# Attention, top-2 experts and a gated feed-forward on one core: sums of gathered outputs on POOL, one token tile's gathers behind the branch, a transpose a step later, and some norm products on ACT

## The chip, the cores and the metric

One core of a Trainium2 chip runs the whole program. Its engines run beside each other, each through its own list of instructions in order: PE (TensorE, matmuls), DVE (VectorE), ACT (ScalarE), POOL (GpSimd) and SP (SyncE, which mostly issues DMAs). They wait for one another by semaphores. The metric is the device time of one execution in microseconds (us), the median of the runs.

## The reference, cut to what matters

```python
# 1. linear attention: 4 batches, 8 heads, 576 positions, 64 per head
kv  = einsum('bhsd,bhse->bhde', k, v)
out = einsum('bhsd,bhde->bhse', q, kv)
x   = out / sqrt(mean(out*out, -1) + 1e-6) * g_norm      # per head
x   = x as 2304 tokens of 512
# 2. eight experts, two for each token
noisy = x @ w_gate + log1p(exp(x @ w_noise)) * noise
top2, w = the two largest of noisy, softmax over the two
y = sum over the two of  w * (relu(x @ w1[e]) @ w2[e])   # 512 -> 1024 -> 512
# 3. a gated feed-forward, 512 -> 1536 -> 512
g = y @ w_gate2
return (g * sigmoid(g) * (y @ w_val)) @ w_out
```

## The kernel before, in words

**Numbers.** Each float32 operand of a large product is split in a high and a low half (names with hi_/lo_, xh/xl, mh/ml, hh/hl, gh/gl), and three matmuls (hi·hi, hi·lo, lo·hi; `three_terms`) take the place of one. ACT makes the high halves, DVE the low ones (lo = value - hi).

**Stages.** The attention (`front`, per batch) leaves unnormalised outputs xo in tiles of 128 tokens, 18 in all. `route_norm` computes the norms ny per token and head on DVE, and POOL multiplies xo by them into xs (L387, two instructions for a row of 128 tokens) and, for the last nine tiles (g = 2), issues the stores of xs to xd in DRAM (L393). Then routing chooses two experts for each token and gives each of its rows a slot (slot_tok).

The experts run in 14 blocks of 256 or 384 rows, eight steps each; a step is one `expert_up` (u), one `expert_act` (hh, hl) and the `expert_down` (y) of the step before. In the first 16 steps the routing of the last nine tiles (`chain`) is woven between the tasks of the steps by `weave`, piece by piece, and PE, ACT, DVE and SP keep the order in which the program is written (PINNED); from step 16 on a scheduler of the compiler orders them. So a different number of instructions in `chain`, or another task in a step, moves where `weave` cuts. A dictionary of tasks says what else is done in a step: `at(step, fn)`. Rows of a block are gathered from xd by POOL's indirect DMAs (`x_gather`, L703); blocks 0 to 3 are transposed by PE (tr, in `x_halves`), later ones by DVE (`turn`, behind a store and a load that reorder quarters: `to_quarters`, L720 and L721).

The feed-forward runs in six groups m of three token tiles, twelve units each: `ffn_up` (ug, uv; sg, a, gh, gl) and `ffn_down` (y('m', m)). For each token tile t, `y_mix` gathers the two expert rows ya and yb from yd (POOL), `y_sum` weights and adds them, and puts the sum out in quarters (yq); `y_get` reads it back; `y_halves` transposes it (`turn` on DVE) and makes mh on ACT and ml on DVE. The gathers of t < 3 read only the rows of the first blocks of each expert.

**The branch.** After unit 1 of the feed-forward, `spill` loads the number of rows that found no slot (toti, L878) into a register on each engine, and each engine branches by it (L879) past a body that handles such rows. With these inputs it is passed. Each engine passes it when it comes to it in its own list.

**Lines.** L387/L393 norm products and stores; L703 gathers; L622 raw weights from DRAM; L630 hi_, L984 lo_ of weights; L669 POOL's adds in the conversion of feed-forward weights (36 in the expert steps); L806 ACT's ya times weight; L807 DVE's yb times weight plus ya; L834 ug and uv; L776 y; L766/L767 hh/hl; L44 is the line of everything recorded in the pinned stretch.

Of the kernel before, what the change touches and what calls it, by code (L numbers as in the profile page):

```python
# [15 lines left out]
AF = mybir.ActivationFunctionType  # L16
OP = mybir.AluOpType
# [32 lines left out]
def attn_moe_ffn(ctx: ExitStack, tc: tile.TileContext, q, k, v, g_norm, w_gate, w_noise, noise, w1, w2,  # L50
                 u_gate, u_val, u_out, out):
    nc = tc.nc
    PE, ACT, V, POOL, SP = (InOrder(tc, e) for e in (nc.tensor, nc.scalar, nc.vector, nc.gpsimd, nc.sync))
    B, H, S, D = q.shape
    NTOK, DM = out.shape
# [3 lines left out]
    P = 128  # L59
# [16 lines left out]
    xd = dram.tile([NTOK, DM], F32, name="xd")  # L76
# [5 lines left out]
    def wtile(nm):  # L82
        return wpool.tile([P, 1024], F32, name=nm, tag="W")
# [22 lines left out]
    def const(shape, dt, nm):  # L106
        return consts.tile(shape, dt, name=nm)
# [64 lines left out]
    wts = const([P, NT, 2], F32, "wts")  # L172
# [182 lines left out]
    def small(shape, nm, dt=F32, most=5):  # L355
        full = [shape[0], most] + shape[2:]
        tag = nm.split("@")[0]
        return pool.tile(full, dt, name=nm, tag="sm_" + tag.split("_")[0], bufs=2 if tag[:2] == "ny" else 1)[:, 0:shape[1]]

    def route_norm(g):  # L360
        ts = list(range(*GRP[g]))
        G = len(ts)
        m = small([P, G, H], f"m@{g}", most=TP)
        V.tensor_scalar(m, SS[g], 1.0 / D, EPS_RMS, op0=OP.mult, op1=OP.add)
        yield
        t1 = small([P, G, H], f"nt@{g}", most=TP)
        V.tensor_scalar(t1.bitcast(I32), m.bitcast(I32), 1, None, op0=OP.logical_shift_right)
        yield
        y = small([P, G, H], f"ny@{g}", most=TP)
        V.tensor_scalar(y.bitcast(I32), t1.bitcast(I32), -1, SEED, op0=OP.mult, op1=OP.add)  # L370
        yield
        for it in range(3):
            V.tensor_mul(t1, y, y)
            yield
            V.scalar_tensor_tensor(t1, t1, -0.5, m, op0=OP.mult, op1=OP.mult)
            yield
            V.scalar_tensor_tensor(y, t1, 1.5, y, op0=OP.add, op1=OP.mult)
            yield
        for t, xo in XO.pop(g):
            n = xo.shape[1]  # L380
            xs = wtile(f"xs{t}")
            for r in range(n):
                xi = xo[:, r].rearrange("p (c s) (l i) -> p c s l i", s=2, i=32)
                xp = xs[:, r * DM:(r + 1) * DM].rearrange("p (s l c i) -> p c s l i", s=2, l=2, i=32)
                yr = y[:, t - ts[0] + r].rearrange("p (c s) -> p c s", s=2)
                for s in range(2):
                    POOL.tensor_mul(xp[:, :, s], xi[:, :, s], yr[:, :, s, None, None].to_broadcast([P, 4, 2, 32]))  # L387
            store = partial((SP if g < 2 else POOL).dma_start, xd[t * P:(t + n) * P].rearrange("(r p) d -> p r d", r=n),
                            xs[:, 0:n * DM].rearrange("p (r d) -> p r d", r=n))
            if g < 2:  # L390
                XO.setdefault(g, []).append(store)
            else:
                store()  # L393
        RT["y", g] = y

    def route_logits(g):
        t0, t1 = GRP[g]
        G = t1 - t0
        y = RT.pop(("y", g))
        lg, az = small([P, G, 16], f"lg@{g}", most=TP), small([P, G, E], f"az@{g}", most=TP)  # L400
        for b in (g,) if g < 2 else (2, 3):
            ts = slice(PART[b][0] - t0, PART[b][1] - t0)
            lz = ZO[b].rearrange("p g h n -> p (g h) n")
            V.tensor_mul(lz, lz, y[:, ts].rearrange("p g h -> p (g h)")[:, :, None].to_broadcast([P, lz.shape[1], 16]))
            yield BIG
            V.tensor_reduce(lg[:, ts], ZO[b].rearrange("p g h n -> p g n h"), op=OP.add, axis=AX.X)
            yield BIG
        zn = lg[:, :, 8:16]
        V.scalar_tensor_tensor(az, zn, -1.0, zn, op0=OP.mult, op1=OP.max)
        yield  # L410
        RT["lg", g] = lg, az
# [306 lines left out]
    def to_quarters(x, nm):  # L718
        put, get = by_quarter(nm)
        SP.dma_start(put, x.rearrange("p (g k) -> p g k", g=4))  # L720
        return lambda: SP.dma_start(x, get)  # L721
# [81 lines left out]

    def y_sum(t):
        a, b = XT.pop(("y", t))
        ACT.activation(a, a, AF.Copy, scale=wts[:, t, 0:1])  # L806
        V.scalar_tensor_tensor(b, b, wts[:, t, 1:2], a, op0=OP.mult, op1=OP.add)  # L807
        XT["y", t] = b, to_quarters(b, f"yq{t}")

    def y_get(t):  # L810
# [166 lines left out]
    def at(step, fn, *args):  # L977
        todo.setdefault(step, []).append((fn, args))
# [35 lines left out]
    for bk in range(2, NB):  # L1014
        p = starts[bk - 1]
        n = blocks[bk][2] // P
        for i in range(n):
            if bk > 2:
                at(p + 1 if bk < 4 else p - 4, x_gather, bk, i)
            if bk > 3:  # L1020
                at(p - 2 + i, x_put, bk, i)
                at(p + 1 + i, x_get, bk, i)
            at(p + (5 if bk == 2 else 4) + i, x_halves, bk, i)
    for m in range(NM):
        p = first_ffn + NU * (m - 1) if m else first_ffn - NF - 4
        for i in range(3):
            lags = [2 * i + d for d in (1, 3, 4, 7)] if m else [i + d for d in (0, 4, 6, 8)]
            for lag, fn in zip(lags, (y_mix, y_sum, y_get, y_halves)):
                at(p + lag, fn, 3 * m + i)

# [17 lines left out]
    def front(b):  # L1048
# [61 lines left out]
        if b < 2:  # L1110
            drain(route_norm(b), route_logits(b))
# [29 lines left out]
    def chain():  # L1141
        yield from route_norm(2)
        yield from route_logits(2)
        yield STOP
        yield BIG
        yield from route_top(2)
        yield from route_rank(2)
        yield from route_rows(2)
        yield from slot_hits(2)
        yield from late_sum()  # L1150
        for i in range(3):
            x_gather(2, i)

    def weave(gen, tasks, budget):

        spent = 0
        for i, task in enumerate(tasks + [lambda: None]):
            while spent < budget * (i + 1) / (len(tasks) + 1):
                spent += next(gen, STOP) or 2
            task()  # L1160

    at(PINNED, mix_weights)
    at(PINNED + 1, y_rows)
    for i in range(2):
# [77 lines left out]
```

## Time and profile before

| what | value |
|---|---|
| runs | 1019.26 us median of 3 (1015.68 to 1022.33) |
| the profiled execution | 1018.99 us, span 1017.3 us |
| mean granted clock of PE | 0.991 |
| busy share of PE, DVE, ACT, POOL | 97%, 55%, 35%, 18% |
| PE's idle time put down to other work, three longest single waits | 3.7, 3.6, 2.1 us |

The span is the time from the first to the last instruction in the trace; 1.7 us of the execution lie around it. Idle time of an engine carries the name of what ended it. A queue name with q (ACTq, PEq) is the engine's sequencer: register loads, branches, DMA issues.

### The profile page before, as it was taken

To read this page: it belongs to the slowest core of one execution; us is meant where nothing else is said; L and a number is where in the kernel's file an instruction comes from. 1 tells how busy PE (TensorE), PEld (TensorE's weight loads), DVE (VectorE), ACT (ScalarE), POOL (GpSimd) and SP (SyncE) were. 2 spreads that over 40 slices of the span, in tenths; PEclk is the share of its full clock that TensorE was granted. 3 is DMA by queue.
4 is the path that set the end of the run, shared out by engine and by line. 5 is a ranking of instruction groups with operands and counts; after the bars stand their busy time and mean duration, and the time that the engine had idled before them with its cause. 6 is when DMAs were issued, how large, how long until landed. Compare 5 with 4: busy or idle time off the path is not lost. (4 is left out here: it accounts for less than half of the span.)

```text
span 1017.3 us, 14793 instructions
## 1 busy us (share of the span) xinstructions
PE 985.5 (97%) x5719; PEld 899.1 (88%) x5720; DVE 564.0 (55%) x1080; ACT 351.6 (35%) x620; POOL 181.4 (18%) x171
## 2 busy tenths in 40 slices
PE   7997899999999999999999899999999999999998
PEld 7885788888989899898889799999999999999997
DVE  1879879877847776678466442522522522522222
ACT  4653434443426253542156321411411411411211
POOL 2416152233121313014120320200200200000000
PEclk9989999999999999999999999999999999999999
DMA  9987678688857768676472620400500500300000
GB/s 249 302 243 199 216 249 287 208 310 259 284 187 226 243 211 284 199 220 208 149 232 95 187 84 1 145 11 1 149 8 1 155 2 1 93 1 1 32 1 32
DMA packets 114508, 151.61 MB, mean 149 GB/s; under 512 B 15936, under 2 KB 75328, under 8 KB 114432
## 3 DMA queue, kind: packets, MB, share of 16 engines
q1 hardware_dynamic: 99536, 113.51, 36.6%
q0 software_dynamic: 6736, 22.29, 7.2%
q10 hardware_dynamic: 8160, 14.81, 4.0%
q8 instruction: 46, 0.75, 0.3%
q14 instruction: 30, 0.25, 0.1%
HBM read 108.64 MB, written 41.94 MB: 148 GB/s over the span
## 5 line engine op out<-in xcount | busy, mean ns | idle before, releaser
L840 DVE TENSOR_TENSOR sg<-ug,sg 128x384 f32<-128x384 f32 x72 | 40.0, 555 | 181.5 <-ACT sg L839 181.4
L757 PE MATMUL u<-xl,hi_w 128*128 128x384 f32 (+1 forms) x448 | 140.4, 313 | 0.0
L757 PE MATMUL u<-xh,lo_w 128*128 128x384 f32 (+1 forms) x448 | 140.3, 313 | 0.0
L757 PE MATMUL u<-xh,hi_w 128*128 128x384 f32 (+1 forms) x448 | 140.2, 313 | 0.0
L776 PE MATMUL y<-hi_w,hh 128*128 128x512 f32 x290 | 115.3, 398 | 2.0 <-ACT hh L766 1.8
L776 PE MATMUL y<-lo_w,hh 128*128 128x512 f32 x290 | 115.0, 396 | 0.0
L834 PE MATMUL ug<-mh,hi_ug 128*128 128x384 f32 x288 | 97.4, 338 | 3.7 <-ACTq L879 3.7
L766 ACT ACTIVATE hh<-u 128x384 fp32r<-128x384 f32 (+1 forms) x113 | 49.4, 438 | 147.6 <-PE u L757 145.3
L834 PE MATMUL ug<-mh,lo_ug 128*128 128x384 f32 x288 | 97.6, 339 | 0.0
L834 PE MATMUL ug<-ml,hi_ug 128*128 128x384 f32 x288 | 97.2, 338 | 0.0
L839 ACT ACTIVATE sg<-ug 128x384 f32<-128x384 f32 x72 | 35.4, 491 | 177.4 <-PE ug L834 175.8
L834 PE MATMUL uv<-mh,lo_uv 128*128 128x384 f32 x288 | 96.6, 335 | 0.0
L776 PE MATMUL y<-hi_w,hl 128*128 128x512 f32 x290 | 95.5, 399 | 1.2 <-DVE hl L767 1.0
L834 PE MATMUL uv<-mh,hi_uv 128*128 128x384 f32 x288 | 96.5, 335 | 0.0
L834 PE MATMUL uv<-ml,hi_uv 128*128 128x384 f32 x288 | 96.4, 335 | 0.0
L757 PEld LDWEIGHTS u<-xl,hi_w 128*128 128x128 f32 x448 | 84.7, 189 | 5.7
L757 PEld LDWEIGHTS u<-xh,lo_w 128*128 128x128 f32 x448 | 84.6, 189 | 5.0
L757 PEld LDWEIGHTS u<-xh,hi_w 128*128 128x128 f32 x448 | 84.6, 189 | 4.6
L843 ACT ACTIVATE gh<-a 128x384 fp32r<-128x384 f32 x72 | 37.8, 525 | 145.5 <-DVE a L841 145.5
L767 DVE SCALAR_TENSOR_TENSOR hl<-u,hh 128x384 fp32r<-128x384 f32 (+1 forms) x113 | 56.0, 496 | 56.2 <-ACT hh L766 56.2
L841 DVE TENSOR_TENSOR a<-uv,sg 128x384 f32<-128x384 f32 x72 | 40.1, 556 | 59.6 <-PE uv L834 59.6
L984 DVE TENSOR_TENSOR lo_w<-raw_w,hi_w 128x1024 fp32r<-128x1024 f32 x48 | 59.8, 1246 | 22.2 <-ACT hi_w L630 20.9
(421 smaller groups left out, 2010.3 us busy)
## 6 DMA issues: line engine op xcount, KB each, us to landing
raw_w<-in_moe_w_dram SPq DMA_DIRECT2D x56, 512.0 KB
yd<-ys ACTq DMA_DIRECT2D x40, 256.0 KB
xq<-xg SPq DMA_DIRECT2D x30, 256.0 KB
xg<-xq SPq DMA_DIRECT2D x30, 256.0 KB
d_ug<-in_moe_w_gate_dram SPq DMA_DIRECT2D x12, 512.0 KB
d_uv<-in_moe_w_val_dram SPq DMA_DIRECT2D x12, 512.0 KB
d_uo<-in_moe_w_out_dram SPq DMA_DIRECT2D x12, 512.0 KB
yq<-yb SPq DMA_DIRECT2D x18, 256.0 KB
```

Source lines behind the costliest of these rows:

```text
L757: PE.matmul(pu, w[a][:, c, (f % 2) * P:(f % 2 + 1) * P], xs[b][:, c, 0:n], start=(k == 0), stop=(k == 11))
L766: ACT.activation(hi.bitcast(F32R), pu, AF.Relu)
L767: V.scalar_tensor_tensor(lo.bitcast(F32R), pu, 0.0, hi, op0=OP.max, op1=OP.subtract)
L776: PE.matmul(ACC[key][i], hs[a][:, i * P:(i + 1) * P], w[b][:, fi], start=(f == 0 and k == 0), stop=(f == nf - 1 and k == 2), skip_group_ch ...
L834: PE.matmul(pu, w[a][:, c, (f % 2) * P:(f % 2 + 1) * P], xs[b][:, c], start=(k == 0), stop=(k == 11))
L839: ACT.activation(sg, ps[0], AF.Sigmoid)
L840: V.tensor_mul(sg, ps[0], sg)
L841: V.tensor_mul(a, ps[1], sg)
L843: ACT.activation(hi.bitcast(F32R), a, AF.Copy)
L984: at(step + 1, lambda: V.tensor_sub(*late.pop()))
```

## The change

Four parts. (1) In `route_norm` for g = 2, tiles 15 (two rows of 128 tokens) and 17 (one row) are no longer multiplied by POOL. `scale_later` queues 24 ACT instructions, one for a row and head (128x64, the norm as its scale operand), and behind each tile's the store by POOL; `scale_some` issues up to five of these items in each of the steps 5 to 12 (the first come in step 6). (2) In `y_sum` ACT's and DVE's instruction give way to three of POOL: two products by the weight as a pointer scalar, and an add. (3) The lags of the feed-forward's tasks for m >= 1 go from (1, 3, 4, 7) to (2, 4, 5, 7), so that the gathers of t = 3, which read all of yd, stand behind the branch. (4) The transposes of block 2 go from steps 13, 14, 15 to steps 14, 15, 15.

```diff
+            if g == 2 and t > 13:
+                at(5 if t == 15 else 9, scale_later, t, xo, y[:, t - ts[0]:t - ts[0] + n], n)
+                continue
...
+    def scale_later(t, xo, y, n):
+        xs = wtile(f"xs{t}")
+        todo_of = []
+        for r in range(n):
...
+            for h in range(H):
+                todo_of.append(partial(ACT.activation, xp[:, h // 2, h % 2], xi[:, h // 2, h % 2], AF.Copy,
+                                       scale=y[:, r, h:h + 1]))
+        todo_of.append(partial(POOL.dma_start, xd[t * P:(t + n) * P].rearrange("(r p) d -> p r d", r=n),
+                               xs[:, 0:n * DM].rearrange("p (r d) -> p r d", r=n)))
+        SCALES.extend(todo_of)
...
+    def scale_some():
+        for fn in SCALES[:5]:
+            fn()
+        del SCALES[:5]
...
     def y_sum(t):
         a, b = XT.pop(("y", t))
-        ACT.activation(a, a, AF.Copy, scale=wts[:, t, 0:1])
-        V.scalar_tensor_tensor(b, b, wts[:, t, 1:2], a, op0=OP.mult, op1=OP.add)
+        for c, y in ((0, a), (1, b)):
+            POOL.tensor_scalar(y, y, wts[:, t, c:c + 1], None, op0=OP.mult)
+        POOL.tensor_add(b, b, a)
...
-            at(p + (5 if bk == 2 else 4) + i, x_halves, bk, i)
+            at(p + (min(6 + i, 7) if bk == 2 else 4 + i), x_halves, bk, i)
...
-            lags = [2 * i + d for d in (1, 3, 4, 7)] if m else [i + d for d in (0, 4, 6, 8)]
+            lags = [2 * i + d for d in (2, 4, 5, 7)] if m else [i + d for d in (0, 4, 6, 8)]
...
+    for step in range(5, 13):
+        at(step, scale_some)
```

**DVE in step 5** of the expert steps: the low half of a weight piece, then the routing chain's polynomial (ac) around hl_4, the low half that PE's y of that step takes. Before:

```order
L44 TENSOR_TENSOR s2@2_1352<-s@2_1350 128x72
L44 TENSOR_TENSOR lo_w_0_3_1360<-raw_w_0_3_1167,hi_w_0_3_1359 128x1024
L44 TENSOR_SCALAR ac@2_1363<-s2@2_1352 128x72
L44 SCALAR_TENSOR_TENSOR ac@2_1363<-ac@2_1363,s2@2_1352 128x72 x4
L44 SCALAR_TENSOR_TENSOR hl_4_1389<-u_4_1333,hh_4_1388 128x256
L44 SCALAR_TENSOR_TENSOR ac@2_1363<-ac@2_1363,s2@2_1352 128x72 x2
```

and with the change:

```order
L44 TENSOR_TENSOR s2@2_1342<-s@2_1340 128x72
L44 TENSOR_TENSOR lo_w_0_3_1350<-raw_w_0_3_1167,hi_w_0_3_1349 128x1024
L44 TENSOR_SCALAR ac@2_1353<-s2@2_1342 128x72
L44 SCALAR_TENSOR_TENSOR ac@2_1353<-ac@2_1353,s2@2_1342 128x72 x3
L44 SCALAR_TENSOR_TENSOR hl_4_1378<-u_4_1323,hh_4_1377 128x256
L44 SCALAR_TENSOR_TENSOR ac@2_1353<-ac@2_1353,s2@2_1342 128x72 x3
```

One of the four ac instructions ahead of hl_4 has moved behind it.

**ACT before the branch**, from the last store of the expert blocks (ys) on; sg_1 and gh_1 are the sigmoid and the high half of unit 1 of the feed-forward. Before:

```order
L789 DMA yd<-ys_1_6001 128x512
L839 ACTIVATE sg_1_6030<-ug_1_6004 128x384
L843 ACTIVATE gh_1_6035<-a_1_6031 128x384
L806 ACTIVATE ya_6040<-ya_6040,wts 128x512
L878 TENSOR_LOAD toti
L879 COMPARE_AND_BRANCH
```

and with the change:

```order
L812 DMA yd<-ys_1_6022 128x512
L863 ACTIVATE sg_1_6051<-ug_1_6025 128x384
L867 ACTIVATE gh_1_6056<-a_1_6052 128x384
L902 TENSOR_LOAD toti
L903 COMPARE_AND_BRANCH
```

The product of the gathered ya of t = 3 no longer stands ahead of ACT's branch.

**POOL around the sums of m = 0** (t = 0 to 2), up to the branch. Before:

```order
L703 DMA ya_5616<-yd,posi 128x512
L703 DMA yb_5617<-yd,posi 128x512
L703 DMA ya_5649<-yd,posi 128x512
L703 DMA yb_5650<-yd,posi 128x512
L703 DMA ya_6040<-yd,posi 128x512
L703 DMA yb_6041<-yd,posi 128x512
L878 TENSOR_LOAD toti
```

and with the change:

```order
L726 DMA ya_5667<-yd,posi 128x512
L726 DMA yb_5668<-yd,posi 128x512
L830 TENSOR_SCALAR ya_5597<-ya_5597,wts 128x512
L830 TENSOR_SCALAR yb_5598<-yb_5598,wts 128x512
L830 TENSOR_SCALAR ya_5634<-ya_5634,wts 128x512
L830 TENSOR_SCALAR yb_5635<-yb_5635,wts 128x512
L830 TENSOR_SCALAR ya_5667<-ya_5667,wts 128x512
L830 TENSOR_SCALAR yb_5668<-yb_5668,wts 128x512
L831 TENSOR_TENSOR yb_5598<-yb_5598,ya_5597 128x512
L831 TENSOR_TENSOR yb_5635<-yb_5635,ya_5634 128x512
L831 TENSOR_TENSOR yb_5668<-yb_5668,ya_5667 128x512
L902 TENSOR_LOAD toti
```

All six products stand ahead of the first add, and the two gathers of t = 3 are gone from ahead of the branch. On DVE the transposes of the three sums (turn) stand later than before: the first directly ahead of the hl_4 of the last expert block, the other two behind it, ahead of its hl_5; before, all three stood behind its hl_0.

## Rows read from the trace of the kernel before

**Rows 1.** page part 1: busy time, its share of the span, instructions

```profile
PE 985.5 (97%) x5719; PEld 899.1 (88%) x5720; DVE 564.0 (55%) x1080; ACT 351.6 (35%) x620; POOL 181.4 (18%) x171
```

**Rows 2.** waits of PE: awaited, then total us, times, longest us

```profile
PE y L44 <- DVE hl L44: 7.5, 7, 3.6
PE ug L834 <- ACTq L879: 3.7, 1, 3.7
...
PE tr L44 <- DMA xg<-xd,slot_tok: 2.1, 1, 2.1
PE y L776 <- ACT hh L766: 1.8, 1, 1.8
```

**Rows 3.** windows: each engine's busy us and count, PEclk (granted clock), DMA share, GB/s

```profile
100.70:104.20 3.50, 3.46 (x12) 3.09 (x13) 3.36 (x12) 0.00 (x0) 3.48 (x6) 0.51 0.71 267
...
150.00:500.00 350.00, 348.90 (x1867) 313.50 (x1866) 262.17 (x445) 136.64 (x202) 90.15 (x62) 1.00 0.74 238
...
525.90:531.00 5.10, 5.09 (x20) 4.34 (x21) 5.10 (x8) 3.57 (x5) 0.00 (x0) 0.67 0.63 177
...
571.40:575.40 4.00, 3.95 (x14) 3.95 (x15) 1.71 (x2) 1.06 (x2) 2.36 (x2) 0.57 0.88 255
575.40:1015.00 439.60, 437.27 (x2298) 408.60 (x2296) 154.45 (x257) 107.95 (x188) 28.89 (x27) 1.00 0.15 46
```

**Rows 4.** timeline of DVE: start, us, work [idle before, what ended it]

```profile
85.06 0.23 DVE L44 SCALAR_TENSOR_TENSOR ny@2_1197<-nt@2_1193,ny@2_1197 128x72 f32<-128x72 f32 x1
...
95.85 1.64 DVE L44 TENSOR_TENSOR lo_w<-raw_w,hi_w 128x1024 fp32r<-128x1024 f32 x1
...
98.06 2.29 DVE L44 SCALAR_TENSOR_TENSOR ac@2_1363<-ac@2_1363,s2@2_1352 128x72 f32<-128x72 f32 x4
100.27 0.41 DVE L44 SCALAR_TENSOR_TENSOR hl<-u,hh 128x256 fp32r<-128x256 f32 x1
...
544.91 0.43 DVE L767 SCALAR_TENSOR_TENSOR hl<-u,hh 128x256 fp32r<-128x256 f32 x1
```

**Rows 5.** timeline of POOL

```profile
86.32 13.94 POOL L387 TENSOR_TENSOR xs<-xo,ny@2_1197 128x256 f32<-128x256 f32 x17 [16.12 <-ACT hh L44]
...
126.82 1.03 POOL L703 DMA_INDIRECT xg<-xd,slot_tok  x1 [22.47 <-DVE slot_tok L44]
...
343.28 3.23 POOL L669 TENSOR_TENSOR f_uv<-f_uv,d_uv 128x512 f32<-128x512 f32 x1 [11.52 <-DVE d_uv L668]
...
518.98 1.05 POOL L703 DMA_INDIRECT yb<-yd,posi  x1 [0.30 <-issue]
```

**Rows 6.** timeline of ACT

```profile
105.38 1.57 ACT L44 ACTIVATE xh<-tr,ghalf 128x256 fp32r<-128x256 f32 x4 [8.24 <-PE tr L44]
...
523.93 0.72 ACT L806 ACTIVATE ya<-ya,wts 128x512 f32<-128x512 f32 x1 [3.21 <-DMA ya<-yd,posi]
...
570.38 0.72 ACT L806 ACTIVATE ya<-ya,wts 128x512 f32<-128x512 f32 x1 [5.67 <-DMA ya<-yd,posi]
572.50 1.06 ACT L630 ACTIVATE hi_ug<-raw_ug 128x1024 fp32r<-128x1024 f32 x1 [1.41 <-DMA raw_ug<-ug]
```

**Rows 7.** timeline of PE, where block 2's inputs are transposed

```profile
132.74 0.66 PE L44 MATMUL tr<-ident,xg 128*128 128x128 f32 x4 [2.09 <-DMA xg<-xd,slot_tok]
```

**Rows 8.** timeline of SP's queue, behind the branch

```profile
567.87 0.37 SPq L622 DMA_DIRECT2D raw_ug<-ug  x1
...
571.91 0.36 SPq L720 DMA_DIRECT2D yq<-yb  x1
...
574.65 0.33 SPq L721 DMA_DIRECT2D yb<-yq  x1
```

**Rows 9.** groups by form: count, busy us, mean ns, idle before and its releasers

```profile
L669 POOL TENSOR_TENSOR f_ug<-f_ug,d_ug 128x512 f32<-128x512 f32 x12 | 22.6, 1890 | 43.5 <-DVE d_ug L668 26.8 <-issue 16.6
...
L168 POOL MEMSET rb<- 128x1280 f32 x4 | 4.5, 1155 | 0.0
...
L44 ACT ACTIVATE zo<-o 128x64 f32<-128x64 f32 x12 | 4.0, 335 | 0.0
```

More of the change, by code (lines that the diff above doesn't have):

```diff
@@ L394, in route_norm @@
         RT["y", g] = y
+    def scale_later(t, xo, y, n):
+        xs = wtile(f"xs{t}")
+        todo_of = []
+        for r in range(n):
+            xi = xo[:, r].rearrange("p (c s) (l i) -> p c s l i", s=2, i=32)
+            xp = xs[:, r * DM:(r + 1) * DM].rearrange("p (s l c i) -> p c s l i", s=2, l=2, i=32)
+            for h in range(H):
[4 more added lines that the diff above has]
+        SCALES.extend(todo_of)
+    SCALES = []
+    def scale_some():
+        for fn in SCALES[:5]:
+            fn()
+        del SCALES[:5]
     def route_logits(g):
```

## The prediction

> **What bounds the kernel now.** I read the busy shares first: PE works in 97% of the span [rows 1], so the kernel ends when PE's list ends, and only PE's idle time and its clock can give anything back. The windows say where there is nothing to find: in 150 to 500 us PE is busy in 348.90 of 350 us, and in 575.4 to 1015 us in 437.27 of 439.6, both at a granted clock of 1.00 [rows 3]. What ACT and DVE lose to POOL's sums from m = 1 on, in that last stretch, is therefore worth nothing. Then the waits of PE: 3.6 us in one piece for a low half hl of DVE, 3.7 for ACT's sequencer at the branch, 2.1 for gathered rows ahead of a transpose, 1.8 for hh of ACT [rows 2]. Last the windows behind three of these waits: the granted clock is 0.51 for 3.5 us, 0.67 for 5.1 us and 0.57 for 4.0 us [rows 3], that is near the lower of the two levels (1.2 of 2.4 GHz) for part of them. Work that would have been done at full clock was thus prolonged by 3.5 × 0.49 = 1.7, 5.1 × 0.33 = 1.7 and 4.0 × 0.43 = 1.7 us. Each of the four edits stands at one of these places.
>
> **A: norm products from POOL to ACT.** The wait of 3.6 us ends with hl_4, which DVE begins at 100.27 [rows 4]. Ahead of it stand a low half of 1.64 us and four ac instructions of 2.29 us, 0.57 each, where an instruction of that shape took 0.23 a little earlier [rows 4]. POOL ran 17 products back to back beside them, 13.94 us from 86.32, 0.82 each [rows 5]. Six of its 18 products go; the twelfth ends at 86.32 + 12 × 0.82 = 96.2. DVE then has POOL beside it only at the start of the low half, which I leave as it is (end 97.5). A first ac instruction and three more (the fourth has moved behind hl_4) at 0.25 each end at 98.5: hl_4 comes 1.8 us sooner, and the wait shrinks to 1.8. Whether the clock falls behind a shorter wait, no row decides; of the 1.7 us I take 0.6. **A = 2.4**, between 0.6 (only the one ac that moves, 0.57, is saved) and 5.3 (wait and clock loss both gone).
>
> ACT gets 24 instructions; the nearest row is zo, 128x64, 335 ns [rows 9], so 8.0 us, five at a time 1.7 us. The first five stand in front of xh, where ACT was idle for 8.24 us [rows 6]; the later ones stand behind a high half of a weight, ahead of an hh. I cost them at nothing; if the cover is short by one group, hh and then hl come up to 1.7 us late in a stretch where hl sets PE's pace. The store of tile 17 is now issued when ACT is through, by my count at about 121 us. POOL's queue behind it holds the gathers of block 2, which begin at 126.82 after a wait of 22.47 for slot_tok [rows 5]. Put to read-back of a tile of sums takes 574.65 - 571.91 = 2.7 us [rows 8], so the store lands at about 124.5, 2 us in hand.
>
> **B: transposes of block 2 a step later.** They start at 132.74 after 2.09 us of waiting [rows 7], 5.9 us after the first gather was issued at 126.82 [rows 5]. A step of two-tile blocks is some 3 us, so one step later the rows are there; what fills the gap is the u and y of the step that PE then does first. The halves of the three tiles must be done before the first u of block 2, with the last two transposes now in one step; I keep 0.3 back for that. **B = 1.8**, between 0 and 2.1.
>
> **C: the weighted ya off ACT, m = 0.** ACT sat 3.21 us until 523.93 in front of a gather's product [rows 6]; behind it stood hh, for which PE waited 1.8 us [rows 2], followed by the window of 0.67 [rows 3]. The product goes to POOL, which nobody waits for yet. What is late next is DVE's hl: it is busy in all of the 5.10 us there [rows 3], but loses three instructions to POOL. **C = 3.2** of 1.8 + 1.7, between 0.5 (DVE takes over as the wait) and 3.5.
>
> POOL's price is not in the trace: no product with a pointer scalar stands there. Below, a memset of 128x1280 takes 1.155 us, 0.46 for 512 columns; above, the adds of 128x512 take 1.89 in the mean [rows 9] and 3.23 in a long one [rows 5]. I take 1.7 for all, nearest the adds. POOL issues its last gather of m = 0 at 518.98 and is free at 520.0 [rows 5]; nine instructions end at 535.3, put and read-back 2 × 2.7 later is 540.8. The last turn is wanted behind hl_4, which started at 544.91 [rows 4], so less C's 3.2, and with hl_4 and two turns, at about 543. It holds up to (543 - 520 - 5.4) / 9 = 2.0 us an instruction.
>
> **D: the gathers of t = 3 behind the branch.** ACT waited 5.67 us for them and began the product at 570.38 [rows 6], 0.72 us, and only then took its branch; PE stood 3.7 us for it [rows 2] and lost 1.7 by the clock [rows 3]. Without the product ACT branches right after gh_1. PE's own passage remains: SP's raw_ug, which needs PE past the branch, was issued at 567.87 [rows 8], within the wait; I keep 0.5 for it. These loads do not move earlier with PE. raw_ug still lands at about 572.5 and hi_ug, of 1.06 us, ends at 573.6 [rows 6], with sg_2 behind it on ACT. From 568 PE has ug and uv of unit 2 and eight y that have moved behind the branch, 32 matmuls at 437.27 / 2298 = 0.19 us [rows 3], till 574, and then ug of unit 3, till 576; a buffer for uv_3 is wanted then, and sg_2 should have freed it by 575. The margin is thin, so I give back 1.1. **D = 3.8** of 5.4, between 1.5 and 5.4.
>
> **Sum.** 2.4 + 1.8 + 3.2 + 3.8 = 11.2 us off the profiled execution's 1018.99 is 1007.8. The median of the three runs is 0.3 above that execution; I say **1008**.
>
> **Rivals.** *R1, POOL's sums hold DVE up in the last expert blocks.* For: beside POOL's products ac took 0.57 instead of 0.23 [rows 4], 0.34 lost in 0.82 of POOL's time. Nine sums of 1.7 would cost DVE 0.41 × 15 = 6 us; three instructions it no longer does and some slack are worth half of that, so PE waits some 3 us and C is gone: 1011. Against: in 150 to 500 us POOL was busy for 90 us, mostly with adds of this shape, and PE missed 1.1 us in all [rows 3]. Chance 0.13. The Trainium skill (SBUF — State Buffer, Who interferes with whom) calls the port pair that DVE and GpSimd share an exclusive lock. By that rule alone the time is R1's; the trace agrees for ac, and for hl, which reads PSUM, it shows 0.41 us even beside POOL [rows 4].
>
> *R2, loads or PE's own passage take the place of ACT's wait.* If sg_2 comes 2 us too late behind hi_ug, D is 1.5: 1010.1. For: SP issues only when PE has passed. Against: the eight moved y. Chance 0.17.
>
> *R3, tile 17's store comes late* and gather and transposes wait as before: B is 0, 1009.6. Against: 2 us in hand. Chance 0.08.
>
> *R4, A does not happen as written*: hl_4 is sooner, but DVE's later chain, or ACT's added groups, make PE wait in the following steps instead, and A nets 0.6: 1009.6. Chance 0.07.
>
> *R5, slower: the sums of m = 0 come late.* On DVE turn stands ahead of hl_4 and hl_5, so a late sum holds up PE at once. It decides from 2.0 us an instruction; at the 3.23 of the long add [rows 5] nine end at 549.1, turn is possible at 554.5 and 11.5 us late, and a clock loss of 1.7 follows: 1007.8 + 13.2 = 1021. Speaking for it: POOL and DVE delay each other just here. Against: the mean of the adds is 1.89 [rows 9]. Chance 0.05.
>
> **Numbers.** The forecast has 0.50, with its own range 1004 to 1010.5. One per cent, about what can be told from no change here, is 10.2 us: faster by more means below 1009.1. Of the forecast's 0.50 some 0.38 lie there, of the 0.45 of R1 to R4, which sit 0.5 to 2 us above, a quarter, 0.11: faster 0.49. Slower by over 1% takes R5 at a still higher price: 0.03. Within 1%: 0.48. The range reaches from 1003, where nearly all upper ends come together (5.3 + 2.1 + 3.5 + 5.4 = 16.3 gives 1002.7), to 1014, for R1 with R2 and a shortfall.
>
> **What would show it.** A: POOL's products end near 96, hl_4 starts near 98.5, the wait for it is under 2 us. B: no wait of tr for xg, or one under 0.3. C: no wait of y for hh near 524, clock 1.00 from 526 to 531. D: PE idle under 1 us at the branch, and no wait for ug or uv's buffers in the 8 us behind it. POOL's products and adds at 1.0 to 2.0 us each, and no turn waiting for yb near 540. The prediction is wrong if PE's wait for hl in the last expert blocks grows, or if turn waits for yb ahead of hl_4.

## The result, and the profile after

The changed kernel takes 1006.5 us, the median of 4 runs (1004.76 to 1007.84), against 1017.47 us for the kernel before on the same chip (4 runs): a ratio of 0.989, 95% interval 0.9863 to 0.9917. Timed again beside a variant, it took 1007.18 against 1017.27 (0.9909, 0.987 to 0.9947). The forecast was 1008, with a range from 1003 to 1014. The profiled execution took 1007.84 us, its span is 1006.1.

To see where the time went I use the **lead of PE**: both kernels run 5719 matmuls in nearly the same order, so the start of the n-th matmul in the trace of before, less its start in another trace, is how far PE is ahead at that place. Its growth between two places is what the stretch gave. The columns name the places by the time of before; they are matmuls that are the same in both lists.

| kernel | lead at 88 us | to 157 | to 518 | to 535 | to 558 | to 578 | to the end | sum from 88 us |
|---|---|---|---|---|---|---|---|---|
| the change | -3.2 | 5.7 | 1.3 | 4.4 | -1.2 | 4.8 | -0.6 | 14.3 |
| the change, second trace | -1.3 | 5.7 | 1.7 | 4.4 | -1.4 | 4.8 | -0.2 | 14.9 |
| e1: part 1 alone | -0.8 | 5.6 | 2.0 | 1.1 | -1.3 | 4.8 | -0.9 | 11.3 |
| e8: its order alone | 0.2 | 2.9 | 1.9 | 1.7 | -1.0 | -0.9 | 0.0 | 4.6 |
| e2: part 2 alone | -0.4 | 1.1 | 0.8 | 4.4 | -1.2 | 4.8 | -2.5 | 7.4 |
| e3: part 3 alone | 0.2 | -2.2 | 1.2 | 1.3 | -1.4 | 4.8 | -0.6 | 3.2 |
| e4: part 4 alone | -1.8 | 2.2 | -1.0 | 1.7 | -1.1 | -0.9 | 0.0 | 0.9 |
| e13: all but part 4 | -3.8 | 4.8 | 1.4 | 4.4 | -1.2 | 4.8 | -0.6 | 13.6 |
| e14: all but part 3 | 0.7 | 5.7 | 0.3 | 4.4 | -1.1 | 4.8 | -1.9 | 12.1 |
| e5: six more POOL products | -2.1 | 5.5 | 1.7 | 4.4 | -6.0 | 5.1 | -0.3 | 10.4 |
| e6: m = 0 by POOL and DVE | -0.7 | 5.7 | 1.3 | 4.4 | -6.4 | 4.8 | -0.3 | 9.5 |
| e7: tile 13 on ACT as well | -2.5 | 6.3 | 1.8 | 4.4 | -1.5 | 4.8 | -0.6 | 15.2 |
| e7, second trace | -0.9 | 6.3 | -0.9 | 4.4 | -2.5 | 4.8 | -0.5 | 11.5 |

(In e5, PE's order differs at 558, so its two entries there are only right together.) Up to 88 us all these kernels run the same list on PE, and still they lie up to 4.5 us apart there, so that much of a span is chance; the stretches behind it repeat within some 0.4 us where the lists agree. The larger exceptions are the stretch to 518 in e14 (0.3) and in the second trace of e7 (-0.9), and that to 558 in the latter (-2.5); they are told below. The change's 14.3 us from 88 us on, less the 3.2 it was behind by then, are the 11.1 us between the two profiled executions.

The page's first part and the longest waits of PE after (answering [rows 1, 2]; awaited, total us, times, longest):

```profile
PE 984.3 (98%) x5719; PEld 898.2 (89%) x5720; DVE 552.5 (55%) x1062; ACT 345.0 (34%) x626; POOL 256.9 (26%) x219
```

```profile
PE y L44 <- DVE hl L44: 5.6, 7, 1.7
...
PE tr L44 <- DMA xg<-xd,slot_tok: 1.1, 1, 1.1
...
PE ug L858 <- PEq L903: 0.4, 1, 0.4
```

No wait is over 1.7 us now. The one for xg is at 75 us, for block 0's rows, ahead of everything that the change touches; the one ahead of block 2 is gone. ACT's sequencer is no longer what PE waits for at the branch: what is left is PE's own passage.

The windows of PE behind the three places where it had waited (answering [rows 3]; busy us of PE, PEld, DVE, ACT and POOL, then the granted clock):

```profile
101.90:105.40 3.50, 3.07 (x20) 2.65 (x20) 3.29 (x14) 0.31 (x1) 0.00 (x0) 1.00 0.89 293
518.00:530.00 12.00, 12.00 (x80) 10.89 (x79) 7.42 (x7) 6.42 (x10) 12.00 (x9) 1.00 0.79 267
559.40:563.40 4.00, 4.00 (x23) 4.00 (x24) 0.00 (x0) 0.86 (x1) 2.88 (x3) 1.00 0.76 242
575.00:1000.00 425.00, 424.75 (x2230) 396.59 (x2229) 137.87 (x234) 92.59 (x165) 84.67 (x66) 1.00 0.15 43
```

The clock is 1.00 in all of them, where it was 0.51, 0.67 and 0.57. The second row lies within the 16 us of POOL's sums of m = 0: POOL works in all of the 12 us and PE in all of them too. In the last row POOL is busy for 85 us and PE misses 0.25 in 425.

DVE around hl_4 (answering [rows 4]; start, us):

```profile
99.03 1.64 DVE L44 TENSOR_TENSOR lo_w<-raw_w,hi_w 128x1024 fp32r<-128x1024 f32 x1
100.60 0.18 DVE L44 TENSOR_SCALAR ac@2_1353<-s2@2_1342 128x72 f32<-128x72 f32 x1
100.82 0.77 DVE L44 SCALAR_TENSOR_TENSOR ac@2_1353<-ac@2_1353,s2@2_1342 128x72 f32<-128x72 f32 x3
101.50 0.42 DVE L44 SCALAR_TENSOR_TENSOR hl<-u,hh 128x256 fp32r<-128x256 f32 x1
```

From the start of the low half to that of hl_4 it is 2.5 us; before it was 4.4. The three ac take 0.26 us each, for POOL's products had ended:

```profile
89.51 10.09 POOL L390 TENSOR_TENSOR xs<-xo,ny@2_1197 128x256 f32<-128x256 f32 x12 [16.48 <-DMA raw_w<-in_moe_w_dram]
...
516.16 2.59 POOL L830 TENSOR_SCALAR ya<-ya,wts 128x512 f32<-128x512 f32 x1
...
527.38 4.77 POOL L831 TENSOR_TENSOR yb<-yb,ya 128x512 f32<-128x512 f32 x3
```

The last two rows are the first product and the three adds of m = 0 (answering [rows 5]): nine instructions in 532.15 - 516.16 = 16.0 us, 1.78 each. Over the whole kernel the groups by form give the prices that no row of before had (count, busy us, mean ns), and that of ACT's norm products:

```profile
L830 POOL TENSOR_SCALAR yb<-yb,wts 128x512 f32<-128x512 f32 x18 | 30.2, 1676 | 0.0
L830 POOL TENSOR_SCALAR ya<-ya,wts 128x512 f32<-128x512 f32 x18 | 29.5, 1638 | 0.2
L831 POOL TENSOR_TENSOR yb<-yb,ya 128x512 f32<-128x512 f32 x18 | 23.6, 1334 | 0.0
L44 ACT ACTIVATE xs<-xo,ny@2_1197 128x64 f32<-128x64 f32 x24 | 6.3, 342 | 0.0
```

DVE beside POOL's products and adds, and at the first turn of m = 0:

```profile
517.57 1.37 DVE L1008 TENSOR_TENSOR lo_uv<-raw_uv,hi_uv 128x1024 fp32r<-128x1024 f32 x1
...
523.06 1.38 DVE L1008 TENSOR_TENSOR lo_ug<-raw_ug,hi_ug 128x1024 fp32r<-128x1024 f32 x1
...
527.23 3.80 DVE L1008 TENSOR_TENSOR lo_uv<-raw_uv,hi_uv 128x1024 fp32r<-128x1024 f32 x1 [1.90 <-ACT hi_uv L653]
...
538.74 0.71 DVE L716 STREAM_TRANSPOSE turn<-yb 128x512 f32<-128x512 f32 x1 [2.46 <-DMA yb<-yq]
```

A low half that takes 1.22 us alone took up to 1.38 beside the products and 3.80 beside the adds, and turn, which stands ahead of hl_4, did wait 2.46 us for its sum. PE was busy through both, but lost 1.2 us a little later (535 to 558 in the table), half of it in a wait for hl_5, where the kernel before had none. PE's row, and SP's queue between POOL's sums and turn (yq<-yb is a put, yb<-yq a read-back):

```profile
544.27 0.50 PE L799 MATMUL y<-hi_w,hl 128*128 128x512 f32 x1 [0.57 <-DVE hl L790]
```

```profile
528.70 0.36 SPq L743 DMA_DIRECT2D yq<-yb  x1
531.05 0.36 SPq L645 DMA_DIRECT2D raw_uo<-uo  x1
531.50 1.04 SPq L743 DMA_DIRECT2D yq<-yb  x2
532.64 5.81 SPq L744 DMA_DIRECT2D yb<-yq  x3
```

The first sum was put out at 528.70, in time. Its read-back was issued only behind the puts of all three sums, at 532.64, and turn could start at 538.74: 10.0 us for put and read-back, where the forecast had 5.4.

### The profile page after: what moved, and what is told of

It reads as the page before. It is cut to its first block, busy times and chain, and to the rows that moved or that the text cites. A ratio compares the mean times of both kernels' runs of the same rounds, so it can differ in the third digit from the quotient of the medians.

```text
span 1006.1 us, 14818 instructions
## 1 busy us (share of the span) xinstructions
PE 984.3 (98%) x5719; PEld 898.2 (89%) x5720; DVE 552.5 (55%) x1062; ACT 345.0 (34%) x626; POOL 256.9 (26%) x219
```

## The experiments

**e1, part 1 alone**: `scale_later` and `scale_some` as in the change, everything else as before.

```diff
+            if g == 2 and t > 13:
+                at(5 if t == 15 else 9, scale_later, t, xo, y[:, t - ts[0]:t - ts[0] + n], n)
+                continue
...
+    for step in range(5, 13):
+        at(step, scale_some)
```

> Only part 1: tiles 15 and 17's norm products by ACT per head, everything else as before. My theory: POOL's shorter list and the ac instruction that moves behind hl_4 shorten PE's wait for hl_4 from 3.6 to about 1.7 us and the lower clock behind it goes: PE is 2.9 to 3.7 us ahead of before at 110 us of the span, against the place where the step began; the waits at 132, 524 and at the branch (2.1, 1.8, 3.7 us) stay. About 1015.5 us. Rival (ACT's added groups make hh late): PE loses 1 us or more again between 105 and 126 us.

Measured 1008.74 us beside 1017.93 for before, one run each. The wait for hl_4 is 1.7 us and the lead grows by 3.1 us from 88 to 109 us, as the theory had it, and nothing is lost up to 126. But the wait for xg at 132 is gone as well, and so is the long one at the branch: two gains that I had put down to other parts. At the branch ACT still has the product in its list; its gather is sooner (answering the third row of [rows 6]):

```profile
560.77 0.72 ACT L829 ACTIVATE ya<-ya,wts 128x512 f32<-128x512 f32 x1 [2.69 <-DMA ya<-yd,posi]
```

ACT waits 2.69 us for it here, not 5.67, and PE only 0.5. What the gather waits for is the last yd stores: they were issued at 553.18 here and the gather at 557.28, 4.1 us later, against 5.5 before, and it was there 3.5 us after its issue, against 5.1. (These two traces do not hold the landing of the stores; in those of e4 and e14 the gather is issued 0.8 us after the last one landed.) Why these transfers were quicker is open.

**e8, part 1's order alone**: empty tasks in place of part 1's, POOL making all products.

```diff
+    for step in range(5, 13):
+        at(step, lambda: None)
     at(PINNED, mix_weights)
...
             n = xo.shape[1]
+            if g == 2 and t > 13:
+                at(5 if t == 15 else 9, lambda: None)
             xs = wtile(f"xs{t}")
```

> The order alone: before, with empty tasks in the steps where part 1 has its tasks, so that DVE's order is that of the change (three ac ahead of hl_4) and POOL still makes all 18 products. If POOL's products set the pace of DVE there, hl_4 comes only one ac, 0.6 us, sooner, the wait is 3.0 us and the clock still falls. If the order was what counted, the wait falls to about 1.7 us as with the whole change.

1014.24 us beside 1017.93. PE's waits and the clock behind the wait for hl_4:

```profile
PE y L44 <- DVE hl L44: 5.8, 5, 3.0
...
PE ug L836 <- ACTq L881: 3.7, 1, 3.7
PE y L778 <- ACT hh L768: 2.0, 1, 2.0
```

```profile
100.00:103.50 3.50, 3.50 (x12) 3.11 (x13) 3.36 (x8) 0.00 (x0) 3.48 (x6) 0.51 0.65 247
```

3.0 us and a clock of 0.51: the order is worth the 0.6 of the one ac. The rest of A, 1.3 us of wait and 1.2 of clock, comes from POOL's six products. But the wait for xg is gone here too, with the transposes at their old steps. In before the packets of the first gather (q0) come late and thin; in the third microsecond from its issue only 13 of them are moved, and in the changed kernel 63 (bytes in MB, then the time the packets took):

```profile
q0 software_dynamic: 13, 0.05, 56.3%
q1 hardware_dynamic: 49, 0.07, 23.0%
```

```profile
q0 software_dynamic: 63, 0.22, 69.2%
q1 hardware_dynamic: 10, 0.04, 13.6%
```

The first block is before, 128.82 to 129.82 us, the second the changed kernel, 128.63 to 129.63. In e8 and e1 the same microsecond holds 64 and 61 packets. There the weight load ahead of the gather was issued 1.41 us before it, in the kernel before 0.96 (SP's raw_w at 125.86, the gather at 126.82). SP's order is the same in all of them here; on DVE one instruction of the routing chain (low) has moved from ahead of a low half of a weight (lo_w) to behind it. That the order is enough is shown by e8; that the load's lead is what quickens the gather is not: in e7 it is 1.7 and 2.1 us, and the first gather takes 5.0 and 4.7 us.

**e13, all but part 4.**

```diff
-            at(p + (min(6 + i, 7) if bk == 2 else 4 + i), x_halves, bk, i)
+            at(p + (5 if bk == 2 else 4) + i, x_halves, bk, i)
```

> The changed kernel without part 4 (block 2's transposes at their old steps). Parts 1 to 3 alone. If DVE's and SP's new order is by itself enough, because the gathers land in about 3.3 us in place of 5.8, the wait of tr for xg stays gone and the lead at 145 us, counted from 88 us, is that of the changed kernel (5.7 us) within 0.3. If the step later is needed beside it, 1.5 to 2 us come back as a wait.

1009.19 us in one run that was 3.8 us behind at 88 us. No wait for xg ahead of block 2. The lead to 157 us grew by 4.8, not 5.7; 0.5 of the difference is a wait for hh at 116 us, which before has too (0.47) and the change has not. Part 1 alone, also without part 4, gained 5.6. So the step later is not needed beside the new order.

**e4, part 4 alone.**

```diff
-            at(p + (5 if bk == 2 else 4) + i, x_halves, bk, i)
+            at(p + (min(6 + i, 7) if bk == 2 else 4 + i), x_halves, bk, i)
```

> Only part 4: block 2's transposes a step later. If the step later is what removes the wait, PE's wait of tr for xg (2.1 us before, 1.6 to 1.8 in the kernels with parts 2 or 3 alone) is gone and PE is 1.6 to 2.1 us further ahead of before at 145 us than at 125 us; the waits at hl_4 (3.6), near 524 (1.8) and at the branch (3.7) stay: about 1016. If it is not, because the last two transposes then hold up the first u of block 2, as much is lost again by 145 us and nothing is left.

1019.8 us beside 1023.5. The wait for xg is gone and the lead grows by 2.2 us to 157: part 4 does by itself what was forecast of it. The sum from 88 us is 0.9, since 1.0 us went again in the middle, at waits of 0.4 to 1.2 us for hh and hl, and the wait at the branch was 3.9. So the time missed the 1016 that was expected.

**e2, part 2 alone**, and **e3, part 3 alone**. The edit of e2, and that of e3:

```diff
-        ACT.activation(a, a, AF.Copy, scale=wts[:, t, 0:1])
-        V.scalar_tensor_tensor(b, b, wts[:, t, 1:2], a, op0=OP.mult, op1=OP.add)
+        for c, y in ((0, a), (1, b)):
+            POOL.tensor_scalar(y, y, wts[:, t, c:c + 1], None, op0=OP.mult)
+        POOL.tensor_add(b, b, a)
```

```diff
-            lags = [2 * i + d for d in (1, 3, 4, 7)] if m else [i + d for d in (0, 4, 6, 8)]
+            lags = [2 * i + d for d in (2, 4, 5, 7)] if m else [i + d for d in (0, 4, 6, 8)]
```

> Only part 2: the sums by POOL, lags as before, so t = 3's gathers still stand ahead of POOL's branch. ACT has no ya product any more, neither near 524 nor ahead of its branch. My theory: what PE waited for in both places was that product in ACT's list, so both waits (1.8 and 3.7 us) and the lower clock behind each go with this part alone, 6 to 8 us in all: about 1012. Rival (the gathers ahead of the branch are what delays it): the wait at the branch stays over 3 us and only 3 to 4 us are gained.

> Only part 3: the lags of the feed-forward's tasks, sums still by ACT and DVE. The product of t = 3 is no longer ahead of ACT's branch: the wait of 3.7 us at the branch falls to about 0.5 and the clock does not fall behind it; the wait near 524 (1.8 us, clock 0.67) stays. 4 to 5 us gained: about 1014. If the gain at the branch needed POOL's sums as well, it would stay over 3 us here.

1011.94 and 1015.5 us, beside 1017.93. Each removes the long wait at the branch by itself, 4.8 us in the table, as part 1 did, and of the two only part 2 the one near 524: PE waits 1.9 us for hh in e3. (The 2.2 us that e3 loses up to 157 us are clock: 0.81 from 104.5 to 110 us and 0.71 from 133.2 to 139, where before had 1.00.) In e2 2.5 us are lost again behind the branch, where raw_ug comes late. ACT's hi_ug there (answering the last row of [rows 6]):

```profile
567.83 1.06 ACT L630 ACTIVATE hi_ug<-raw_ug 128x1024 fp32r<-128x1024 f32 x1 [7.86 <-DMA raw_ug<-ug]
```

sg_2 stands behind it in ACT's list, and PE waited 0.7 us for a buffer of uv and 1.0 for gh.

**e14, all but part 3.**

```diff
-            lags = [2 * i + d for d in (2, 4, 5, 7)] if m else [i + d for d in (0, 4, 6, 8)]
+            lags = [2 * i + d for d in (1, 3, 4, 7)] if m else [i + d for d in (0, 4, 6, 8)]
```

> The changed kernel with the old lags (1, 3, 4, 7): the gathers of t = 3 and a product of POOL stand ahead of POOL's branch. If taking ACT's product away is enough, PE waits under 0.6 us at the branch, as with part 2 alone; but raw weights then come later behind it and 2 to 3 us are lost in the 25 us behind the branch, as there, against 0.6 in the changed kernel. If the lags matter for nothing else, the loss behind the branch is 0.6 as well.

1006.37 us, 0.7 ahead at 88 us. To 518 it gained only 0.3, with waits of 0.64 and 0.34 us for hl at 232 and 463. At the branch PE waits 0.45 us; behind it 1.9 us are lost, with the same two waits (0.55 and 0.7). That, against 0.6 and 0.2, is what part 3 is worth beside part 2: some 1.5 us.

**e5, six more POOL products**, for t < 3.

```diff
         for c, y in ((0, a), (1, b)):
+            if t < 3:
+                POOL.tensor_scalar(y, y, 1.0, None, op0=OP.mult)
             POOL.tensor_scalar(y, y, wts[:, t, c:c + 1], None, op0=OP.mult)
```

> The changed kernel with six more POOL products for t = 0 to 2 (each of the two gathered tiles multiplied by 1 first, computing the same): 15 instructions of about 1.7 us in place of nine. If late sums of m = 0 hold PE up, as the fifth rival has it: POOL is through some 10 us later, near 542, the last turn is possible near 548, and PE loses 4 to 9 us ahead of the feed-forward's first unit or in the last expert steps: 1010 to 1017. If there were slack for ten more us, nothing changes: about 1007.

1010.72 us beside 1023.5. POOL ends at 541.3, and PE waits 3.68 us for the mh of the last sum, with the clock at 0.59 behind it:

```profile
549.49 0.69 PE L860 MATMUL ug<-mh,hi_ug 128*128 128x384 f32 x1 [3.68 <-ACT mh L847]
```

```profile
549.50:553.50 4.00, 4.00 (x14) 3.73 (x15) 1.03 (x1) 0.00 (x0) 0.00 (x0) 0.59 0.00 0
```

In the table 6.0 us are lost there, 4.8 more than in the change: the fifth rival's mechanism. POOL is through 9.1 us later than in the change, of which PE waited 3.68, so in this order some 5.5 us were to spare (an estimate from these two numbers). The compiler's scheduler had moved turn behind hl_6 for it, so the sums hold up the feed-forward's first unit and not hl_4.

**e6, the sums of m = 0 by POOL and DVE.**

```diff
-        for c, y in ((0, a), (1, b)):
-            POOL.tensor_scalar(y, y, wts[:, t, c:c + 1], None, op0=OP.mult)
-        POOL.tensor_add(b, b, a)
+        if t < 3:
+            POOL.tensor_scalar(a, a, wts[:, t, 0:1], None, op0=OP.mult)
+            V.scalar_tensor_tensor(b, b, wts[:, t, 1:2], a, op0=OP.mult, op1=OP.add)
+        else:
...
```

> The changed kernel with, for t = 0 to 2 alone, ya by POOL and the rest by one DVE instruction as before. In the changed kernel DVE's low half took 3.80 us beside POOL's three adds, and PE lost 1.7 us between 540 and 550 when turn stood ahead of hl. If POOL's late sums and its adds beside DVE cost that, here no low half in 515 to 540 takes over 2 us, turn comes before 540 without waiting, and PE keeps its lead there: 1.5 us less than the changed kernel, about 1006. If it was the place in DVE's list and not the sums, the loss stays.

1010.73 us. No low half between 515 and 540 takes over 1.4 us, so the 3.80 was POOL's adds. But PE loses 6.4 us. DVE and PE there:

```profile
530.72 0.71 DVE L716 STREAM_TRANSPOSE turn<-yb 128x512 f32<-128x512 f32 x1 [6.13 <-DMA yb<-yq]
```

```profile
534.66 0.80 PE L799 MATMUL y<-hi_w,hl 128*128 128x512 f32 x1 [4.74 <-DVE hl L790]
```

```profile
519.93 1.33 SPq L743 DMA_DIRECT2D yq<-yb  x2
...
526.62 0.33 SPq L744 DMA_DIRECT2D yb<-yq  x1
```

With the sums sooner the scheduler put the second turn sooner too, ahead of an hl. But the put of its sum, issued at 519.93, landed only at 526.61; the read-back followed at once and landed at 530.63. So turn was not held up by a late sum: a slow transfer, and the place of turn ahead of an hl, cost more than the adds. The expected 1006 was missed by 4.7 us.

**e7, tile 13 on ACT as well**, in two runs, and the change beside the second.

```diff
-            if g == 2 and t > 13:
-                at(5 if t == 15 else 9, scale_later, t, xo, y[:, t - ts[0]:t - ts[0] + n], n)
+            if g == 2 and t > 11:
+                at({13: 5, 15: 7}.get(t, 9), scale_later, t, xo, y[:, t - ts[0]:t - ts[0] + n], n)
...
-        for fn in SCALES[:5]:
+        for fn in SCALES[:8]:
             fn()
-        del SCALES[:5]
+        del SCALES[:8]
```

> The changed kernel with tile 13's products given to ACT as well (40 ACT instructions, up to eight a step; POOL keeps eight). If POOL's products beside DVE set the time of hl_4, its wait falls from 1.7 to under 0.6 us: PE is 1 to 1.5 us further ahead at 110 us than in the changed kernel, counted from 88 us. If ACT's groups of 8 (2.1 us) make hh late, that is lost again by 126 us. About 1006.

> The kernel with tile 13's products on ACT as well, timed. In its one look PE gained 15.2 us on before between 88 us and the end, the changed kernel 14.3, 0.9 us apart, while the stretch ahead of 88 us, which is the same in all kernels, differed by up to 3.4 us from run to run. Expected: some 1 us below the changed kernel, about 1.2% below before, and not to be told from the changed kernel in five rounds.

> The changed kernel as it is, timed on the same chip beside e7_five: ratio to before 0.986 to 0.992, as measured first.

The wait for hl_4 falls to 0.7 us and the lead to 157 us is 6.3 instead of 5.7. Over five rounds e7 took 1007.0 us (0.9892, 0.9858 to 0.9927) and the change 1007.18 (0.9909, 0.987 to 0.9947), both against 1017.27. Not to be told apart; of the 0.9 us between the first traces nothing is left in the second. There e7 lost 0.9 us between 157 and 518, with waits of 0.8 and 0.4 us for hh near 206 and 212 and of 0.5 for hl near 235, and 2.5 us between 535 and 558, with one of 1.79 us for hl, where the third read-back of m = 0 landed at 541.56. Both traces of e7 also wait 2.5 and 2.7 us for block 0's rows near 78 us, ahead of the place where the table's sums begin; the other traces wait there for 0 to 1.6. Why is open.

## Why the prediction was right, point by point

**The sum** came out where it was put: 1007.8 from the profiled execution, 1007.84 measured. That is closer than it deserves. From 88 us on the change gave 14.3 us, not 11.2; the 3.2 us by which this execution was behind before anything of the change ran made up for it. The parts do not add up: alone they give 11.3 + 7.4 + 3.2 + 0.9 = 22.8 us, since parts 1, 2 and 3 each remove the wait at the branch, and parts 1 and 4 each that for xg. No run leaves part 1 or part 2 out of the whole.

**A, 2.4 us**: about 3.1. The mechanism was right as written: POOL's products end sooner, the three ac run at 0.26, the wait is 1.7 (1.8 forecast). The term was too small because I took 0.6 of the clock's 1.7 us; with the shorter wait the clock did not fall, in any trace of part 1. e8 says how it divides: 0.6 from the order, 2.5 from POOL. ACT's 24 products were free, as costed (342 ns, against 335).

**B, 1.8**: about 2.5 us between 109 and 157, and right as to part 4's effect (e4: 2.2). But the step said that the gathers take 5.9 us and the transposes move past them. In the changed kernel the first lands in 3.6 us (3.8 in the second trace), because the order of DVE moved (e8), and the wait would have been gone without part 4 (e1, e8, e13). I had looked at the moved order for hl_4 alone, and not asked what else it moves.

**C, 3.2**: 3.2 net, made of 4.4 and -1.2. The 4.4 is against an execution of before in which the clock fell to 0.67 behind this wait; in e1, e3, e4 and e8, which still have a wait of 1.4 to 2.0 us there, the clock stayed at 1.00 and the same stretch gave 1.1 to 1.7. But they lost 1.0 to 1.4 behind it, as the change does, and net they are at -0.2 to 0.7. So with part 2 the place is worth about 3 us.

POOL's price, 1.7 us taken, was 1.78 in that stretch, and POOL was through within 1 us of the forecast: 535.3, less the 3.8 us of PE's lead at 518, is 531.5, and it was 532.15. What the prediction had wrong is put and read-back, 5.4 us taken from two rows behind the branch: they took 10.0 us for the first sum and 8.8 for the last, which was back at 540.96. Why is not shown; a weight load (raw_uo) was issued just ahead of two of the puts, and those took 5.9 us each. So turn waited 2.46 us for yb until 538.74, ahead of hl_4, and PE's wait for hl in the last expert blocks grew from none to 0.57 us. Both are what the prediction named as signs that it is wrong: the forecast of a free turn failed, and the time came out because it cost PE so little. The kernels with the old sums (e1, e3, e4, e8) wait 0.5 to 0.9 us for hl in that stretch as well. With the same nine instructions it was 1.79 us in the second trace of e7.

**D, 3.8**: 4.8 at the branch less 0.6 (0.2 in the second trace) behind it, 4.2. PE's passage was 0.45 us, as the 0.5 kept for it. ACT's hi_ug did wait 4.77 us for raw_ug, but the 32 matmuls covered sg_2, as argued, so of the 1.1 that I gave back about half was needed. The name of the part was wrong: taking the product off ACT (part 2) and moving the gathers (part 3) each do it, part 1 did it too (e1), and what part 3 adds is the loads behind the branch, 1.5 us (e14).

**The middle, 1.3 us**, had no term. In before there are waits of 0.46 and 0.58 us for hl in it, at 238 and 469 us; in the change the longest is 0.21. Such waits, of 0.4 to 1.2 us for hl and hh, come and go between 200 and 480 us, and not by the scheduler's order alone: e7's two traces, of one kernel with the same order on PE, have 1.8 and -0.9. What decides it stays open.

**The rivals.** R1 was half there: DVE was held up, by 2.6 us in one instruction (3.80 against 1.22), but PE was not, since the next hl was not yet wanted. The Trainium skill (SBUF — State Buffer, Who interferes with whom), which calls the shared port pair an exclusive lock, agrees with the 3.80, and with hl's 0.41 us beside the same adds. It does not agree with the low halves beside POOL's products: POOL was busy without a gap and they took 1.37 and 1.38 us, not longer by a whole product. Its rule tells what an overlap can cost DVE, and not whether PE waits for it. R2 did not come about with part 3, and did without it (e2, e14). R3 and R4 did not happen: tile 17's store was issued at 121.01 us, as counted, 5.6 us ahead of the gather, and landed at 125.33, with 1.3 us in hand and not 2. R5 stands under C: not POOL's price, but the transfers behind it brought its signs.

## What to carry to other kernels

A gain is counted by stretches of the trace, at matmuls that both kernels share, since a sum that fits can hide a lucky start. Where a scheduler or a weave decides the order, a part of a change works through the order that it moves as well as through what it takes away: a kernel with empty tasks in its place tells the two apart. And when several parts remove the same wait, each looks like its cause; only leaving one out shows what it is worth.

## What the runs showed that was not expected

- **The length of a wait of about 2 us did not decide whether the clock fell.** Behind 88 us, waits of 3.0 to 4.7 us of PE were followed by a granted clock of 0.50 to 0.64 over the next 3.5 to 4 us in every trace that has one (before, e2, e3, e4, e5, e6, e8). Behind waits of 1.4 to 2.1 us it stayed at 1.00 in before (2.09, for xg), e2 (1.64, for xg), e7's second trace (1.79, for hl), e1, e3, e4 and e8 (for hh), and fell to 0.67 in before (1.78, for hh) and to 0.71 in e3, behind the 1.83 us for xg. Behind the 1.67 us of the change it never fell. As a term of a sum a fall is about 1.7 us, but it can last twice as long: in e8 the clock is 0.50 from 564.3 to 571.1, and 0.9 us more than in before are lost there.
- **How much of the change's gain is clock differs from execution to execution.** One execution of before, of the twelve timed beside e7, took 1010.07 us at a mean granted clock of 0.999; a single stretch of 3.4 us at 0.50 takes 0.0017 off the mean. So in that one the clock can't have fallen as in the trace, for 3.4 us behind each of two waits of over 3 us; whether it had those waits, no trace of it shows. The change took 1004.13 and 1004.76 us at the same mean, 5.3 to 5.9 less. At a mean of 0.994 the two kernels are 9 to 10 us apart (1015.62 and 1016.18 against 1006.25 and 1006.75).
- **POOL's product by a pointer scalar costs more than its add of two tiles**: 1.64 to 1.68 us in the mean, 1.55 for the quickest of them in a row, against 1.33 for the add, both 128x512.
- **The first 30 us differ by chance.** In the changed kernel's trace the granted clock was 0.56 between 10 and 20 us, in that of before 1.00, with the same instructions on PE; the lead at 88 us ran from 0.7 to -3.8.
